# ScalarE's order of two instructions in the expert layers: the copy of the fifth product and the cast of the first activation block

## Chip, cores and metric

One core of a Trainium2 chip runs the whole program. The metric is the device time of one execution in microseconds (us), lower is better.

## The reference

Attention over 4 batches, 8 heads, 768 positions and head size 64, with 4 sink positions and a window of 128, gives 3072 rows `x` of 512 columns. A soft assignment of rows to 8 experts (`P`, eight rounds of row and column scaling) weighs what the experts make of every row:

```python
for e in range(E):                 # 8 experts
    h = np.maximum(x @ w1[e], 0.0) # 512 -> 1024
    ye = h @ w2[e]                 # 1024 -> 512
    out += P[:, e:e + 1] * ye
```

## The kernel before, in words

Every matrix product is made in pieces: an operand is split into a rounded part and the rest, and three of the four partial products are summed in PSUM. The expert layers run over the 3072 rows in three parts of 1024. The first part is interleaved with other work; the second and third part, from 938 us on, are the loop that the change touches. There the work is cut into 32 units for each part (8 experts, 4 slices of 256 hidden columns), so 64 units in all, and both layers use a scheme with seven products of blocks (M1 to M7) in place of eight.

The order is written by hand. `unit` (L1339) goes through the list `STEPS2`, and `tick` runs one step at a time:

```python
STEPS2 = ["M2", "M1", "M5", S_, "M3", S_, "M6", S_, S_, "M7", S_, S_, "M4", S_]
```

Steps are counted from 0 below. A step with a product's name is six matmuls of the first layer (`product`, L721) into one of two PSUM tiles. M2, M5 and M3 go to the tile `c2`, and M3 adds to what M5 left there; M1, M6, M7 and M4 go to `c1`. A step `S_` is a step of the second layer (L1269) with products made of earlier units' activations: six matmuls, or three where a group of one unit is worked on (group [0] and [1] at the start of each part; unit 3 takes two such steps in each `S_`).

What follows a product is issued in `after`. After M2, M5 and M3, ScalarE copies `c2` to SBUF (`copied`, L1215, tiles M). After M1, M6 and M7, VectorE adds that copy to `c1` (L1219, `summed`), applies relu and the expert's weight (L1220) and so makes the activation blocks A11, A21 and A22 in tiles `w`; after M4 it makes A12 (L1249). GpSimd makes three more blocks S3, S1, S2, S4 out of these by sums and differences (L1238, L1242, L1243, L1251; the last makes S4 in the place of A11, one step into the next unit).

Each of the seven blocks is then split into `hf` tiles for the second layer by `form` and `piece`: ScalarE casts the block (L746), and one step later VectorE subtracts the cast from the block (L747). `form(steps, ...)` sets by `at` how many steps after the current one the cast is issued; what is due at a step is issued ahead of the step's own work, in the order in which it was put on the list. S4's cast, put on the list in step 12 of a unit with 5 steps, comes due in step 3 of the next one.

Engines work through their own instructions in the order in which they are issued. M3's first matmul writes `c2` and so waits until ScalarE has copied M5 out of it.

Of the kernel before, what the change touches and what calls it, by code (L numbers as in the profile page):

```python
# [220 lines left out]
def tile_sink_attention_moe(ctx: ExitStack, tc: tile.TileContext, q, k, v, wg, w1, w2, out):  # L221
# [496 lines left out]
    def product(ps, w1, x, start, stop):  # L718

        for j, (a, k, b) in enumerate(TERMS):  # L720
            nc.tensor.matmul(ps, lhsT=w1(a, k), rhs=x[:, b, k, :], start=(start and j == 0),  # L721
                             stop=(stop and j == len(TERMS) - 1), skip_group_check=not start)
# [9 lines left out]
    def at(steps, f):  # L732
        due.setdefault(clock[0] + steps, []).append(f)
# [10 lines left out]
    def piece(dst, src, then=None):  # L744

        nc.scalar.copy(dst[:, 0], src)  # L746
        at(1, lambda: nc.vector.tensor_sub(dst[:, 1], src, f32(dst[:, 0])))  # L747
        if then:
            at(3, then)
# [392 lines left out]
    with ExitStack() as p1:  # L1142
# [12 lines left out]
        def load_w1(k):  # L1155
            for _ in range(k):
                key = next(coming1, None)
                if key:
                    part, n, m = key
                    t = W1Q[key] = w1p.tile([P, 2, KH, P], F32R, name="W1q")  # L1160
                    nc.sync.dma_start(f32(t).rearrange("p w k f -> p w (k f)"), w1s[units1[n]][:, FA[W1_OF[m]]])
# [28 lines left out]
        def load_form(m):  # L1190
            fm = READS[m]
            XF[fm] = (xpool if fm[0] == "B" else xtp).tile([P, 2, KH, HT], F32R, name=fm)
            nc.sync.dma_start(f32(XF[fm]), xfs[FORMS.index(fm)])
# [3 lines left out]
        def first2(part, n):  # L1197

            PB = PBS[part, units1[n][0]]
            T = {}  # L1200

            def run(m):
                c = "c2" if m in ("M2", "M5", "M3") else "c1"
                start = m in ("M2", "M1", "M5")
                if start:
                    T[c] = ps0.tile([P, HT], F32, name=c)
                W = W1Q.pop((part, n, m))
                product(T[c], lambda a, k: W[:, a, k, :], XF[READS[m]], start, True)
                at(1, lambda: load_w1(1))
                if (part, n) == (1, NJ - 1):  # L1210
                    at(1, lambda: load_form(m))

            def copied(m):
                t = T[m] = cp.tile([P, HT], F32, name=m)
                nc.scalar.copy(t, T["c2"])  # L1215

            def summed(key, m, th):
                w = T[key] = wp.tile([P, HT], F32, name="w")
                nc.vector.tensor_add(w, T["c1"], T[m])  # L1219
                nc.vector.scalar_tensor_tensor(w, w, 0.0, PB[:, th], op0=ALU.max, op1=ALU.mult)  # L1220

            def form(steps, fm, src):
                def f():
                    t = F[part, n, fm] = hp.tile([P, 2, HT], F32R, name="hf")
                    piece(t, src)

                at(steps, f)

            def after(m):
                if m in ("M2", "M5", "M3"):  # L1230
                    copied(m)
                elif m == "M1":
                    summed("A11", "M2", 0)
                    form(1, "A11", T["A11"])
                elif m == "M6":
                    summed("A21", "M3", 1)
                    S3 = wp.tile([P, HT], F32, name="w")
                    nc.gpsimd.tensor_sub(S3, T["A11"], T["A21"])  # L1238
                    form(2, "S3", S3)
                elif m == "M7":  # L1240
                    summed("A22", "M5", 1)
                    nc.gpsimd.tensor_add(T["A21"], T["A21"], T["A22"])  # L1242
                    nc.gpsimd.tensor_sub(T["A11"], T["A21"], T["A11"])  # L1243
                    form(2, "S1", T["A21"])
                    form(3, "A22", T["A22"])
                    form(4, "S2", T["A11"])
                else:
                    w = wp.tile([P, HT], F32, name="w")
                    nc.vector.scalar_tensor_tensor(w, T["c1"], 0.0, PB[:, 0], op0=ALU.max, op1=ALU.mult)  # L1249
                    form(1, "A12", w)  # L1250
                    at(3, lambda: nc.gpsimd.tensor_sub(T["A11"], w, T["A11"]))  # L1251
                    form(5, "S4", T["A11"])

            return run, after
# [156 lines left out]
```

## Time and profile before

| what | value |
|---|---|
| time, median of 3 runs (lowest to highest) | 2230.27 us (2229.29 to 2231.7) |
| the profiled execution's own time | 2228.16 us |
| its span in the trace | 2226.4 us |
| TensorE's mean granted clock, share of 2.4 GHz | 0.996 |
| busy share of the span: TensorE matmul, weight load, VectorE, ScalarE, GpSimd | 98%, 80%, 71%, 40%, 33% |
| mean HBM traffic | 204 GB/s |

The profiled execution is one run; 1.8 us of its time lie outside the span. Busy shares are means over stages that differ; a matmul's end is modelled, so how long a step takes is read from the starts of the steps that follow each other.

### The profile page before, as it was taken

How to read it: one execution, taken by the hardware profiler on the slowest of the kernel's cores; microseconds unless marked ns; L12 is line 12 of the kernel's file. 1: busy time of each engine (PE TensorE's matmuls, PEld its weight loads, DVE VectorE, ACT ScalarE, POOL GpSimd, SP SyncE). 2: the span in 40 equal slices, each digit the busy share in tenths (PEclk: the TensorE clock that was granted, in tenths of full speed). 3: DMA queues.
4: the chain of work that ended last, by engine and by line, in shares of the span. 5: the costliest groups of instructions: out<-in, count | busy, mean ns of one | idle time of the engine just before them, and what ended most of it. 6: DMA issues, size and time to landing. Idle time of an engine off the chain costs nothing. (4 is left out here: it accounts for less than half of the span.)

```text
span 2226.4 us, 31975 instructions
## 1 busy us (share of the span) xinstructions
PE 2176.1 (98%) x10525; PEld 1770.8 (80%) x10525; DVE 1580.4 (71%) x2941; ACT 889.9 (40%) x1908; POOL 727.0 (33%) x947
## 2 busy tenths in 40 slices
PE   7999998999999999999999999999999999999998
PEld 5888886788888888767888888888778888888886
DVE  8878868687777777767666666666766666666666
ACT  7777753344444444432223333232332333322232
POOL 7655632233233233022222223322222223232221
PEclk9999998999999999999999999999999999999999
DMA  6333325599989989876666666667856666666662
GB/s 173 85 83 82 89 64 175 186 311 298 295 292 305 297 290 304 272 250 194 190 198 200 195 190 200 203 189 253 290 171 197 200 195 190 200 204 190 199 190 82
DMA packets 396635, 454.88 MB, mean 204 GB/s; under 512 B 99696, under 2 KB 263728, under 8 KB 395568
## 3 DMA queue, kind: packets, MB, share of 16 engines
q1 hardware_dynamic: 396464, 452.77, 65.5%
q8 instruction: 86, 1.41, 0.3%
q14 instruction: 85, 0.70, 0.1%
HBM read 315.21 MB, written 137.46 MB: 203 GB/s over the span
## 5 line engine op out<-in xcount | busy, mean ns | idle before, releaser
L746 ACT CAST hf<-w 128x512 fp32r<-128x512 f32 x448 | 271.9, 621 | 722.2 <-POOL w L1238 307.4
L1269 PE MATMUL o<-hf,W2q 128*128 128x512 f32 x1920 | 479.5, 392 | 3.5 <-ACT w L1327 1.7
L1269 PEld LDWEIGHTS o<-hf,W2q 128*128 128x128 f32 x1920 | 359.9, 188 | 84.5 <-DVE acc L1280 2.7
L747 DVE TENSOR_TENSOR hf<-w,hf 128x512 fp32r<-128x512 f32 x448 | 334.0, 762 | 84.6 <-ACT hf L746 71.5
L721 PE MATMUL c<-T,W1q 128*128 128x512 f32 x1536 | 391.7, 390 | 1.7 <-DVE w L1219 1.7
L721 PEld LDWEIGHTS c<-T,W1q 128*128 128x128 f32 x1536 | 287.7, 188 | 65.8 <-DVE w L1219 3.4
L1280 DVE TENSOR_TENSOR acc<-o,acc 128x512 f32<-128x512 f32 x320 | 219.7, 687 | 152.7 <-PE o L1269 152.6
L721 PE MATMUL c<-B,W1q 128*128 128x512 f32 x1152 | 292.3, 397 | 8.5 <-DVE w L1249 3.9
L721 PEld LDWEIGHTS c<-B,W1q 128*128 128x128 f32 x1152 | 210.8, 188 | 78.0 <-ACT M L1215 27.4
L1238 POOL TENSOR_TENSOR w<-w 128x512 f32<-128x512 f32 x64 | 83.0, 1297 | 552.8 <-DVE w L1220 552.8
L1219 DVE TENSOR_TENSOR w<-c,M 128x512 f32<-128x512 f32 x192 | 132.1, 688 | 169.9 <-PE c L721 168.1
L1269 PE MATMUL held<-hf,W2q 128*128 128x512 f32 x768 | 197.8, 392 | 1.2 <-DMA W2q<-w2s 1.2
L721 PE MATMUL c<-T,W1f 128*128 128x512 f32 x672 | 173.3, 394 | 0.0
L992 PE MATMUL o<-W2f,h 128*128 128x512 f32 x672 | 171.4, 391 | 0.8 <-DVE acc L999 0.8
L992 PE MATMUL held<-W2f,h 128*128 128x512 f32 x672 | 171.9, 390 | 0.0
L1269 PEld LDWEIGHTS held<-hf,W2q 128*128 128x128 f32 x768 | 144.1, 188 | 32.5 <-DMA W2q<-w2s 1.6
L1215 ACT COPY M<-c 128x512 f32<-128x512 f32 x192 | 112.2, 585 | 137.9 <-PE c L721 137.9
L1251 POOL TENSOR_TENSOR w<-w 128x512 f32<-128x512 f32 x64 | 107.2, 1675 | 175.4 <-DVE hf L747 175.4
L721 PEld LDWEIGHTS c<-T,W1f 128*128 128x128 f32 x672 | 127.1, 190 | 28.7 <-DVE C L964 0.7
L992 PEld LDWEIGHTS o<-W2f,h 128*128 128x128 f32 x672 | 126.0, 188 | 28.7 <-DVE acc L999 1.2
L992 PEld LDWEIGHTS held<-W2f,h 128*128 128x128 f32 x672 | 126.1, 188 | 26.6
L1242 POOL TENSOR_TENSOR w<-w 128x512 f32<-128x512 f32 x64 | 82.9, 1295 | 184.9 <-DVE w L1220 182.1
(187 smaller groups left out, 3059.8 us busy)
## 6 DMA issues: line engine op xcount, KB each, us to landing
W1q<-w1s SPq DMA_DIRECT2D x448, 256.0 KB
W2q<-w2s SPq DMA_DIRECT2D x448, 256.0 KB
w1s<-W1f SPq DMA_DIRECT2D x56, 896.0 KB
w2s<-WT SPq DMA_DIRECT2D x136, 256.0 KB
r<-in_moe_w_dram SPq DMA_DIRECT2D x64, 512.0 KB
w2s<-W2f SPq DMA_DIRECT2D x56, 256.0 KB
PB<-psd SPq DMA_DIRECT2D x16, 512.0 KB
w2s<-W2f SPq DMA_DIRECT2D x56, 128.0 KB
```

The lines of the kernel that those rows point to most:

```text
L721: nc.tensor.matmul(ps, lhsT=w1(a, k), rhs=x[:, b, k, :], start=(start and j == 0), stop=(stop and j == len(TERMS) - 1), skip_group_check=n ...
L746: nc.scalar.copy(dst[:, 0], src)
L747: at(1, lambda: nc.vector.tensor_sub(dst[:, 1], src, f32(dst[:, 0])))
L992: nc.tensor.matmul(o, lhsT=h[c, th][:, a, off:off + P], rhs=W2F[n][:, w, c, :], start=(begin and c == 0 and j == 0), stop=(end and c == 1 ...
L1215: nc.scalar.copy(t, T["c2"])
L1219: nc.vector.tensor_add(w, T["c1"], T[m])
L1238: nc.gpsimd.tensor_sub(S3, T["A11"], T["A21"])
L1242: nc.gpsimd.tensor_add(T["A21"], T["A21"], T["A22"])
L1251: at(3, lambda: nc.gpsimd.tensor_sub(T["A11"], w, T["A11"]))
L1269: nc.tensor.matmul(o, lhsT=W2Q[part, n, m][:, a, k * P:(k + 1) * P], rhs=F[part, n, H_OF[m]][:, w, :], start=(j == 0 and (begin or not hol ...
L1280: nc.vector.tensor_add(sums[m, k], o, sums[m, k])
```

## The change

```diff
@@ def after(m): @@
                 elif m == "M1":
                     summed("A11", "M2", 0)
-                    form(1, "A11", T["A11"])
+                    form(2, "A11", T["A11"])
```

A11 is made after M1 (step 1). Its cast on ScalarE comes due in step 3 instead of step 2, and VectorE's subtraction in step 4 instead of step 3. The change holds for all 64 units; nothing is added or taken out.

On ScalarE, unit 16 of the second part, from the copy of M2 to the copy of M3. `w_13625` is A11 of this unit, `w_13455` is S4 of the unit before, `c2` is the PSUM tile. Before:

```order
L746 CAST hf_13592<-w_13585 128x512
L1215 COPY M2_13613<-c2_13606 128x512
L746 CAST hf_13630<-w_13625 128x512
L1215 COPY M5_13639<-c2_13632 128x512
L746 CAST hf_13641<-w_13455 128x512
L1215 COPY M3_13659<-c2_13632 128x512
```

With the change:

```order
L746 CAST hf_13592<-w_13585 128x512
L1215 COPY M2_13613<-c2_13606 128x512
L1215 COPY M5_13637<-c2_13630 128x512
L746 CAST hf_13639<-w_13455 128x512
L746 CAST hf_13641<-w_13625 128x512
L1215 COPY M3_13659<-c2_13630 128x512
```

The cast of A11 moved past the copy of M5 and past the cast of S4, and now stands just ahead of the copy of M3.

On VectorE, the same unit, from A11's sum (L1219, L1220) to A21's. Before:

```order
L1219 TENSOR_TENSOR w_13625<-c1_13618,M2_13613 128x512
L1220 SCALAR_TENSOR_TENSOR w_13625<-w_13625,PB_13120 128x512
L747 TENSOR_TENSOR hf_13630<-w_13625,hf_13630 128x512
L747 TENSOR_TENSOR hf_13641<-w_13455,hf_13641 128x512
L1280 TENSOR_TENSOR acc_11171<-o_13663,acc_11171 128x512
L1219 TENSOR_TENSOR w_13681<-c1_13618,M3_13659 128x512
```

With the change:

```order
L1219 TENSOR_TENSOR w_13625<-c1_13618,M2_13613 128x512
L1220 SCALAR_TENSOR_TENSOR w_13625<-w_13625,PB_13120 128x512
L747 TENSOR_TENSOR hf_13639<-w_13455,hf_13639 128x512
L747 TENSOR_TENSOR hf_13641<-w_13625,hf_13641 128x512
L1280 TENSOR_TENSOR acc_11171<-o_13663,acc_11171 128x512
L1219 TENSOR_TENSOR w_13681<-c1_13618,M3_13659 128x512
```

The subtraction for A11 moved behind that for S4; both now stand in step 4, ahead of the second layer's addition of step 5 (L1280).

## Rows read from the trace of the kernel before

**Rows 1.** The page: busy time of each engine, share of the span, instructions.
```profile
PE 2176.1 (98%) x10525; PEld 1770.8 (80%) x10525; DVE 1580.4 (71%) x2941; ACT 889.9 (40%) x1908; POOL 727.0 (33%) x947
```
**Rows 2.** Busy time by stretch, 28 units of the second part: us, busy (instructions), granted clock.
```profile
core 0: us, PE busy (x) PEld busy (x) DVE busy (x) ACT busy (x) POOL busy (x), PEclk, DMA share, GB/s
1015.90:1560.00 544.10, 544.10 (x2354) 439.48 (x2353) 363.09 (x533) 162.27 (x280) 155.94 (x112) 1.00 0.66 203
```
**Rows 3.** Who waited for whom, weight loads, whole span: us, times, longest us.
```profile
PEld c L721 <- ACT M L1215: 28.2, 64, 1.1
```
**Rows 4.** Who waited for whom, matmuls, 760 to 2200 us.
```profile
PE c L721 <- ACT M L1215: 1.8, 4, 0.7
```
**Rows 5.** Timeline, unit 16: start us, duration us, engine, line [idle before <-releaser].
```profile
1249.08 2.88 PE L721 MATMUL c<-B,W1q 128*128 128x512 f32 x12
...
1250.50 1.67 POOL L1251 TENSOR_TENSOR w<-w 128x512 f32<-128x512 f32 x1 [2.43 <-DVE hf L747]
1250.69 0.59 ACT L1215 COPY M<-c 128x512 f32<-128x512 f32 x1 [0.81 <-PE c L721]
1251.57 1.32 PEld L721 LDWEIGHTS c<-T,W1q 128*128 128x128 f32 x6
1251.80 1.52 PE L721 MATMUL c<-T,W1q 128*128 128x512 f32 x6
...
1253.15 1.53 PE L1269 MATMUL held<-hf,W2q 128*128 128x512 f32 x6
1253.52 0.62 ACT L746 CAST hf<-w 128x512 fp32r<-128x512 f32 x1 [2.24 <-DVE w L1220]
1254.04 0.58 ACT L1215 COPY M<-c 128x512 f32<-128x512 f32 x1
1254.17 0.69 DVE L747 TENSOR_TENSOR hf<-w,hf 128x512 fp32r<-128x512 f32 x1 [0.69 <-ACT hf L746]
1254.52 0.62 ACT L746 CAST hf<-w 128x512 fp32r<-128x512 f32 x1
1254.67 1.23 PEld L721 LDWEIGHTS c<-B,W1q 128*128 128x128 f32 x6 [0.41 <-ACT M L1215]
1254.67 1.66 PE L721 MATMUL c<-B,W1q 128*128 128x512 f32 x6
...
1256.17 1.53 PE L1269 MATMUL o<-hf,W2q 128*128 128x512 f32 x6
1256.42 0.59 ACT L1215 COPY M<-c 128x512 f32<-128x512 f32 x1 [1.28 <-PE c L721]
...
1257.74 0.69 DVE L1280 TENSOR_TENSOR acc<-o,acc 128x512 f32<-128x512 f32 x1 [1.88 <-PE o L1269]
...
1258.92 2.91 PE L1269 MATMUL o<-hf,W2q 128*128 128x512 f32 x12
1259.19 0.69 DVE L1219 TENSOR_TENSOR w<-c,M 128x512 f32<-128x512 f32 x1 [0.76 <-PE c L721]
...
1261.67 0.62 PE L721 MATMUL c<-T,W1q 128*128 128x512 f32 x2
```
**Rows 6.** Timeline, last unit of the third part.
```profile
2179.15 1.54 PE L1269 MATMUL o<-hf,W2q 128*128 128x512 f32 x6
...
2180.67 1.23 PEld L721 LDWEIGHTS c<-B,W1q 128*128 128x128 f32 x6 [0.41 <-ACT M L1215]
```
**Rows 7.** Timeline of PE, units 1 and 2 of the second part.
```profile
965.35 1.56 PE L721 MATMUL c<-B,W1q 128*128 128x512 f32 x6
966.74 0.86 PE L1269 MATMUL o<-hf,W2q 128*128 128x512 f32 x3
...
981.72 0.86 PE L1269 MATMUL o<-hf,W2q 128*128 128x512 f32 x3
983.24 1.65 PE L721 MATMUL c<-B,W1q 128*128 128x512 f32 x6 [0.66 <-ACT M L1215]
```
**Rows 8.** Timeline of PE, unit 3 of the second part.
```profile
999.43 0.85 PE L1269 MATMUL held<-hf,W2q 128*128 128x512 f32 x3
...
1001.20 1.66 PE L721 MATMUL c<-B,W1q 128*128 128x512 f32 x6 [0.24 <-ACT M L1215]
1002.70 0.63 PE L1269 MATMUL o<-hf,W2q 128*128 128x512 f32 x2
```

## Prediction

> **What bounds the kernel now.** The page's engine line comes first: TensorE has matmuls in flight for 98% of the span and no other engine is busy for more than 80% [rows 1]. In 28 units of the second part the matmul time fills the stretch to the last hundredth, at a granted clock of 1.00, which is the 2.4 GHz level [rows 2]; by that view nothing is left to win. But a matmul's end is modelled, so I go to the starts. The 28 units take 544.10 us, 19.43 us each.
>
> The list of waits names a cause. TensorE's weight loads waited 64 times, 28.2 us together, for ScalarE's copy of a product (L1215) [rows 3], while the matmul row of the same pair shows 1.8 us in 4 waits [rows 4]. Which of the two is the loss has to come from the timeline of one unit [rows 5]. The reader should follow four step starts there. M2 and M1 are two product steps, 1249.08 to 1251.80: 1.36 us each. Two second-layer steps, 1258.92 to 1261.67, are 1.38 us each. So a second-layer step and a product step should be 2.74 us together. The pair that contains M3 goes from 1253.15 to 1256.17: 3.02 us. **0.28 us are lost there in each unit**: M3 starts 1.52 us after the step ahead instead of 1.38 (0.14), and its own step takes 1.50 instead of 1.36 (0.14).
>
> Why it starts late stands beside it. M3's first weight load starts at 1254.67 and waited for the copy of M5. That copy ran from 1254.04 for 0.58 us. It was ready sooner, but ScalarE was at the cast of A11, which waited for VectorE's L1220 and started at 1253.52. An instruction that nobody needs soon stands ahead of one that TensorE waits for.
>
> **The change, part by part.** The diff adds and removes no instruction and no transfer. It moves 64 casts (ScalarE) and the 64 subtractions behind them (VectorE) by one step; the queue of the DMAs (SyncE) keeps its order.
>
> *The copy of M5.* Without the cast ahead of it, it waits for M5's last matmul alone. Two rows price that wait: M3's copy starts at 1256.42, when M3's step has given way to the next at 1256.17, so 0.25 us later; M2's copy starts at 1250.69, and M2's step ended at 1249.08 + 1.36 = 1250.44, again 0.25. For M5 that is 1253.15 + 0.25 = 1253.40, 0.64 earlier than now. The copy takes 0.59, to 1253.99; from a copy's end to the weight load that waits for it are 0.05 us (1254.62 to 1254.67), so the load may start from 1254.04. In undisturbed steps it starts 0.23 ahead of its matmul (1251.57 for 1251.80). M3 should start at 1253.15 + 1.38 = 1254.53, its load at 1254.30. **The copy is 0.26 us early, so all 0.28 us come back.** The kernel has a twin of this place already: M2, one step between, then M5, which also waits for a copy out of `c2`; M5's first load at 1251.57 shows no wait [rows 5].
>
> *How many units.* The last unit of the third part shows the same 0.41 us of idle ahead of the load, and M3 again 1.52 us behind the step ahead [rows 6]. Each part has three units that differ, 1 to 3; the other 29 of each part show 0.14 us of late start within 0.01. So 58 x 0.28 = 16.2 us.
>
> *Unit 2* has a short second-layer step of three matmuls between M5 and M3, from 981.72; M3 starts at 983.24 [rows 7]. The new copy runs from 981.97 to 982.56, the load and M3 go at 982.61: 0.63 us won, and a part of the wait stays. The third part repeats it: 2 x 0.63 = 1.3 us. *Unit 3*: step from 999.43, M3 at 1001.20, end 1002.70 [rows 8], so 3.27 us for 2.74: 0.53 lost. The copy would end at 1000.27, with 0.05 to the load 1000.32; the load's place is 1000.58, so all comes back: 2 x 0.53 = 1.1 us. *Unit 1* shows no such loss (M3 at 965.35, next step 1.39 later [rows 7]): nothing.
>
> *The cast of A11, one step later.* It costs ScalarE nothing new. After the copy of M5 come the cast of S4 and that of A11. S4's sum on GpSimd is done at 1250.50 + 1.67 = 1252.17, so both casts run at once, 0.6 us each, from 1253.99 to 1255.2; M3's copy has its product at 1256.1 and finds ScalarE idle (it sat idle 1.28 us before that copy [rows 5]). The second layer first reads a unit's A11 in the next unit or later, so nobody waits for the cast.
>
> *The subtraction on VectorE.* 0.69 us move into step 4, where the next work is the addition L1280 at 1257.74, ahead of which VectorE sat idle for 1.88 us for want of TensorE's result [rows 5]. That idle time covers it and 1.2 us remain. If the cover were gone, L1280 would be late; its tile `o` has a second buffer, so it is next written in the second of the two steps from 1258.92, at 1260.3, and the addition now ends at 1258.43: 1.9 us more.
>
> *The sum.* 16.2 + 1.3 + 1.1 = 18.6 us, taken as 18.5. Unknown is how much another wait gives back. Ends for it: nothing, as for M5 after M2's copy, and 2 us, if the few waits in units 1 to 3, where ScalarE also copies second-layer sums, shift by as much as the two kinds of unit above lose (1.3 + 1.1, rounded). I take nothing, since 58 of 64 units are of the first kind. The starts are read to 0.01 us, so 0.28 may be 0.26 to 0.30, or 1.2 us either way in all. The profiled execution took 2228.16 us, and would take 2209.7. The median of the runs stands 2.1 us above it: **2211.8 us.**
>
> **A rule weighed against a row.** M3's first weight load starts with its matmul at 1254.67, not 0.23 ahead of it as elsewhere [rows 5], so the wait holds the load too, and the step behind it is 0.14 us long. The Trainium skill, "TensorE: Matmul & The Clock Gate", section "Step-by-step: what each phase is for", says that TensorE pulls weight loads ahead of matmuls in flight when they go to the background buffer. By that rule the weights would lie ready during the wait, and the 0.14 us in M3's own step would have another cause that the change does not touch. The row speaks against it here.
>
> **Rivals.**
> *Only the late start comes back.* If M3's 1.50 us were a property of its operands, 58 x 0.14 = 8.1, with 1.3 and 2 x 0.39 = 0.8 from units 2 and 3, would be won: 10.2 us, 2220.1. For it: the long steps are all M3's. Against: M2 and M1 read B blocks too at 1.36, and M3 of unit 1, which did not wait, took 1.39 [rows 7]. The rule of the Trainium skill just named belongs here. Chance 0.06.
> *TensorE is full already.* If matmul busy time were the truth, only its 1.8 us of waits could be won [rows 4]: 2228.5. Against: equal steps at equal clock that differ by 0.14. A chance of 0.04, with the case that some new wait eats the gain.
> *Slower: M3's copy becomes the late one.* The cast of A11 and that of S4 now both stand ahead of M3's copy, whose result VectorE adds at 1259.19 for A21 [rows 5]. If GpSimd's S4 came late, both casts and the copy would queue behind it, A21 would be late, and M7, which needs `c1`, with it. S4 would have to end after 1256.1 - 1.2 = 1254.9 instead of 1252.17 for the copy to be late at all, 2 us beyond that for A21's sum to feel it, and 1.5 beyond that for M7, due at 1261.67, when A21's sum has read `c1` by 1259.9. That makes 2.7 + 2 + 1.5 = 6.2 us; at 7.2, 1 us in each unit, less the 0.28: 64 x 0.7 = 45 us, 2275. Against: S4 stood ahead of M3's copy before too, and 2.7 us are a wide margin. Chance 0.02.
> *The change does nothing.* ScalarE's order as built shows the copy ahead of both casts; I give this none of its own.
>
> **How the numbers follow.** The forecast has a chance of 0.88. Its range: 18.6 and 1.2 more, or 1.2 + 2 less, and about 1 us for where the median of three runs falls, so 2209.0 to 2216.0; this alone holds eight in ten, the rivals lie outside. A measurement of this kernel tells 0.2%, 4.5 us, from no change. Faster by more: 0.88 + 0.06 = 0.94; within: 0.04; slower: 0.02.
>
> **What would show it.** In the profile after, the wait of weight loads for L1215 falls from 28.2 us in 64 waits to under 3 us in a few, those of unit 2. Twenty-eight units take 28 x 19.15 = 536 us. In one unit M5's copy starts 0.25 us after the next step begins, two casts follow it back to back, and M3's load starts 0.23 us ahead of its matmul. I would be wrong if the load waited for something else at the same place, if M3's step stayed at 1.50, or if the units stayed at 19.43 with the wait gone.

## The result, and the profile after

| | before | with the change |
|---|---|---|
| median of the runs (lowest to highest) | 2229.78 us of 4 (2226.2 to 2231.7) | 2208.2 us of 4 (2207.69 to 2211.3) |
| profiled execution, its span | 2228.16 us, 2226.4 us | 2211.3 us, 2209.6 us |

The ratio is 0.9912, with a 95% interval of 0.9900 to 0.9924: the change makes the kernel faster by 17 to 22 us. The forecast was 2211.8 us, the range 2209.0 to 2216.0. The direction and the place were right; the median lies 0.8 us under the range's lower end.

The time came back where M3 waited. This is the changed kernel's timeline of the unit shown in [rows 5] (start us, duration us, engine, line, idle before):

```profile
1246.66 2.88 PE L721 MATMUL c<-B,W1q 128*128 128x512 f32 x12
...
1249.38 1.52 PE L721 MATMUL c<-T,W1q 128*128 128x512 f32 x6
...
1250.74 1.54 PE L1269 MATMUL held<-hf,W2q 128*128 128x512 f32 x6
1250.99 0.59 ACT L1215 COPY M<-c 128x512 f32<-128x512 f32 x1 [2.13 <-PE c L721]
1251.48 1.14 ACT L746 CAST hf<-w 128x512 fp32r<-128x512 f32 x2
1251.89 1.32 PEld L721 LDWEIGHTS c<-B,W1q 128*128 128x128 f32 x6
1252.11 1.52 PE L721 MATMUL c<-B,W1q 128*128 128x512 f32 x6
1252.13 1.29 DVE L747 TENSOR_TENSOR hf<-w,hf 128x512 fp32r<-128x512 f32 x2 [1.06 <-ACT hf L746]
...
1253.47 1.54 PE L1269 MATMUL o<-hf,W2q 128*128 128x512 f32 x6
1253.73 0.59 ACT L1215 COPY M<-c 128x512 f32<-128x512 f32 x1 [1.11 <-PE c L721]
...
1255.05 0.69 DVE L1280 TENSOR_TENSOR acc<-o,acc 128x512 f32<-128x512 f32 x1 [1.62 <-PE o L1269]
```

The copy of M5 starts 0.25 us after the step behind M5 begins (1250.74, 1250.99) and ends at 1251.58. M3's first load starts at 1251.89, 0.22 ahead of its matmul and without a wait. From 1250.74 to 1253.47 the pair with M3 takes 2.73 us, where it took 3.02. Both casts follow the copy as one row, both subtractions as another, ahead of the addition L1280, for which VectorE still sits idle for 1.62 us.

The same over 28 units, unit 4 to 31 of the second part, answers to [rows 2]:

```profile
core 0: us, PE busy (x) PEld busy (x) DVE busy (x) ACT busy (x) POOL busy (x), PEclk, DMA share, GB/s
1017.06:1552.80 535.74, 535.74 (x2354) 441.57 (x2353) 361.85 (x533) 162.52 (x280) 155.99 (x112) 1.00 0.67 205
```

That is 19.13 us a unit instead of 19.43, at the same granted clock of 1.00. Matmul busy time fills both stretches to the last hundredth, 544.10 of 544.10 us and 535.74 of 535.74, while 1.5% of the time vanished. The Trainium skill says in "Perfetto Trace Analysis", section "Identifying the Most-Contended Engine", that matmul busy time is a bad measure of how close a kernel is to its limit, and names the share of the peak arithmetic rate and the busy share of weight loads to use instead. The trace agrees: matmul busy time shows nothing of the gain, while the busy share of weight loads rose from 80.8% (439.48 of 544.10) to 82.4% (441.57 of 535.74).

The waits of weight loads for L1215, 28.2 us in 64 before [rows 3], are all but gone. Of the 64, 62 were M3's first load and two were M5's in unit 2; the four that are left are M5 and M3 in unit 2 of each part. The largest waits of first-layer loads in the loop now belong to other lines, with 5.6 and 3.4 us already there before (us, times, longest):

```profile
PEld c L721 <- DVE w L1249: 5.6, 4, 1.4
...
PEld c L721 <- DVE w L1219: 3.5, 5, 1.3
...
PEld c L721 <- ACT M L1215: 1.7, 4, 0.5
```

One part of the profile after is chance. This execution took 3 us more than the other three, and its timeline shows where: the first twelve matmuls of the second part took 5.46 us, not about 3, while the first weights of that part were landing.

```profile
937.78 5.46 PE L721 MATMUL c<-B,W1q 128*128 128x512 f32 x12 [2.81 <-DMA W1q<-w1s]
```

The next profile of the same kernel did not repeat it (unit 0 took 20.7 us there, 21.0 before the change, 23.5 here). Nor does it go with ScalarE's order: unit 0 lies between 20.7 and 23.5 us in the twelve profiles below, and took 22.5 in E2, whose order on ScalarE is that of before. To keep such things out, the profiles are compared below from the first matmul of M2 in unit 1 of the second part to the end of the span, a stretch that holds 63 of the 64 units.

| kernel | span | M2 of unit 1 | from there to the end |
|---|---|---|---|
| before | 2226.4 | 959.0 | 1267.4 |
| changed | 2209.6 | 961.3 | 1248.3 |
| changed, second profile | 2206.7 | 958.9 | 1247.8 |
| changed, third profile | 2208.0 | 959.9 | 1248.1 |
| E1 copy first only | 2206.3 | 958.3 | 1248.0 |
| E2 subtraction late only | 2226.0 | 958.5 | 1267.5 |
| E3 cast twice | 2266.6 | 959.3 | 1307.3 |
| E4 half a cast first | 2212.6 | 958.9 | 1253.7 |
| E5 S1 later | 2205.6 | 960.5 | 1245.1 |
| E6 A11 after M3's copy | 2206.4 | 957.9 | 1248.5 |
| E7 S3 later | 2206.1 | 961.2 | 1244.9 |
| E8 S1, S3, A12 later | 2198.5 | 959.4 | 1239.1 |

The changed kernel repeats within 0.5 us in the last column ("the column" from here on), so differences of 1 us can be read in it.

### The profile page after: what moved, and what is told of

The parts are those of the page before. It is cut to its first block, busy times and chain, and to the rows that moved or that the text cites. A ratio compares the mean times of both kernels' runs of the same rounds, so it can differ in the third digit from the quotient of the medians.

```text
span 2209.6 us, 31976 instructions
## 1 busy us (share of the span) xinstructions
PE 2161.0 (98%) x10525; PEld 1777.6 (80%) x10525; DVE 1578.6 (71%) x2941; ACT 890.4 (40%) x1908; POOL 726.5 (33%) x947
## 5 line engine op out<-in xcount | busy, mean ns | idle before, releaser
L746 ACT CAST hf<-w 128x512 fp32r<-128x512 f32 x448 | 266.3, 622 | 580.1 <-POOL w L1238 306.6
L747 DVE TENSOR_TENSOR hf<-w,hf 128x512 fp32r<-128x512 f32 x448 | 328.7, 761 | 66.2 <-ACT hf L746 57.6
L1280 DVE TENSOR_TENSOR acc<-o,acc 128x512 f32<-128x512 f32 x320 | 220.0, 688 | 180.5 <-PE o L1269 180.3
L721 PE MATMUL c<-B,W1q 128*128 128x512 f32 x1152 | 286.5, 393 | 6.7 <-DVE w L1249 3.9
L721 PEld LDWEIGHTS c<-B,W1q 128*128 128x128 f32 x1152 | 217.1, 189 | 55.3 <-DVE w L1249 5.6
L1219 DVE TENSOR_TENSOR w<-c,M 128x512 f32<-128x512 f32 x192 | 132.3, 689 | 145.1 <-PE c L721 141.3
L1215 ACT COPY M<-c 128x512 f32<-128x512 f32 x192 | 112.9, 588 | 262.7 <-PE c L721 262.7
```

Of the source, the lines that this page charges most:

```text
L1280: nc.vector.tensor_add(sums[m, k], o, sums[m, k])
```

## Experiments

The theory: the cast of A11 ahead of the copy of M5 on ScalarE is the whole cause. The rivals: the move of the subtraction on VectorE did it, or M3's long step belongs to its operands. The two halves of the change were made alone first.

**E1: the copy first, nothing else.** The cast follows the copy in the same step, ahead of S4's cast; VectorE's order is that of before.

```diff
                 if m in ("M2", "M5", "M3"):
                     copied(m)
+                    if m == "M5":
+                        form(0, "A11", T["A11"])
                 elif m == "M1":
                     summed("A11", "M2", 0)
-                    form(1, "A11", T["A11"])
...
-                at(steps, f)
+                at(steps, f) if steps else f()
```

> Only ScalarE's order of the copy of M5 and the cast of A11 is exchanged; the cast follows the copy at once, ahead of S4's cast, and VectorE's subtraction stays in step 3 as before the change. Theory (the cast ahead of the copy is the whole cause): the same gain as the changed kernel, 18 to 21 us, so 2209 to 2212 us, M3's pair of steps 2.74 us. Rival (the move of the subtraction on VectorE, or A11 going behind S4, gives a part): less than 14 us of gain, above 2216 us.

2209.54 us, ratio 0.9911 (0.9894 to 0.9928), 1248.0 us in the column: all of the gain. The copy of M5 again ran without the cast ahead of it:

```profile
1247.94 0.59 ACT L1215 COPY M<-c 128x512 f32<-128x512 f32 x1 [2.13 <-PE c L721]
1248.42 1.14 ACT L746 CAST hf<-w 128x512 fp32r<-128x512 f32 x2
1248.84 1.32 PEld L721 LDWEIGHTS c<-B,W1q 128*128 128x128 f32 x6
```

**E2: the subtraction late, nothing else.**

```diff
-    def piece(dst, src, then=None):
+    def piece(dst, src, then=None, wait=1):
...
-        at(1, lambda: nc.vector.tensor_sub(dst[:, 1], src, f32(dst[:, 0])))
+        at(wait, lambda: nc.vector.tensor_sub(dst[:, 1], src, f32(dst[:, 0])))
...
-                    piece(t, src)
+                    piece(t, src, wait=2 if fm == "A11" else 1)
```

> Only VectorE's subtraction for A11 is moved one step later; ScalarE's order is that of before the change. Theory: no gain, 2230 us within 3 us, 64 waits of weight loads for the copy of M5 as before. Rival (the move on VectorE helps by itself): 5 us or more faster.

2227.77 us, ratio 0.9993 (0.9984 to 1.0003), and the same row of waits for L1215 as before the change:

```profile
PEld c L721 <- ACT M L1215: 28.2, 64, 1.1
```

The step is later in all 64 units, but VectorE's order differs only in the 32 whose step 3 has an addition for VectorE: there the subtraction now stands behind it. In the others, unit 16 among them, nothing lies between steps 3 and 4 on VectorE, and the order is that of before. E2 also leaves A11's subtraction ahead of S4's, which the change does not. What closes this is E1: its order on VectorE is that of before in every unit, and it has the whole gain. So no part of the gain needs the move on VectorE.

**E3: the cast twice.** If the copy's place is the cause, more work ahead of it must cost more.

```diff
                     t = F[part, n, fm] = hp.tile([P, 2, HT], F32R, name="hf")
+                    if fm == "A11":
+                        nc.scalar.copy(t[:, 0], src)
                     piece(t, src)
```

> The cast of A11 stands ahead of the copy of M5 as before the change, and is made twice (the second writes the same values). Theory: a second cast pushes the copy back by the 0.52 us that lie between the starts of a cast and of the copy behind it (1253.52, 1254.04), and as the load of M3 is late already, TensorE loses all of it: 0.80 us a unit instead of 0.28, 62 x 0.52 = 32 us more, 2262 us (2255 to 2268). Rival (M3's long pair of steps is a property of its operands, not of the copy): 2230 us within 3 us.

2268.54 us, ratio 1.0175 (1.0158 to 1.0192). The sign and the place are those of the theory; the size is 0.5 us over the end of what I expected, and the rows say why:

```profile
1262.50 1.54 PE L1271 MATMUL held<-hf,W2q 128*128 128x512 f32 x6
1262.86 0.62 ACT L1226 CAST hf<-w 128x512 fp32r<-128x512 f32 x1 [2.29 <-DVE w L1220]
1263.52 0.62 ACT L746 CAST hf<-w 128x512 fp32r<-128x512 f32 x1
1264.04 0.58 ACT L1215 COPY M<-c 128x512 f32<-128x512 f32 x1
...
1264.67 1.23 PEld L721 LDWEIGHTS c<-B,W1q 128*128 128x128 f32 x6 [1.07 <-ACT M L1215]
```

The second cast starts 0.66 us behind the first, not 0.52. It writes the same tile, and it starts only after the first has ended (1262.86 + 0.62 = 1263.48), where two casts into different tiles overlap by 0.10 us (1.14 us for two of 0.62 in E1). The load of M3 is that much later, and a unit takes 20.07 us (28 units in 561.90) instead of 19.43, 0.64 more.

**E4: half a cast ahead.** A dose between nothing and the whole.

```diff
                     t = F[part, n, fm] = hp.tile([P, 2, HT], F32R, name="hf")
-                    piece(t, src)
+                    if fm == "A11":
+                        nc.scalar.copy(t[:, 0, 0:HT // 2], src[:, 0:HT // 2])
+                        at(1, lambda: nc.vector.tensor_sub(t[:, 1], src, f32(t[:, 0])))
+                    else:
+                        piece(t, src)
...
                     copied(m)
+                    if m == "M5":
+                        t = F[part, n, "A11"]
+                        nc.scalar.copy(t[:, 0, HT // 2:], T["A11"][:, HT // 2:])
```

> The cast of A11 is cut in two: 256 of 512 columns ahead of the copy of M5, the rest behind it; the subtraction is where it was before the change. Theory: a half cast takes some 0.3 us of ScalarE ahead of the copy, so M3's load is about 0.17 us late instead of 0.37; the loss falls to between 0.05 and 0.15 us a unit: 8 to 15 us of gain, 2215 to 2222 us. A rival in which any cast ahead of the copy costs the whole wait gives 2230; one in which the 0.26 us of lead that I worked out are too small a figure gives 2210.

2214.46 us, ratio 0.9935 (0.9918 to 0.9951): 15.5 us of gain by the medians, half a microsecond past what I expected, 13.7 by the column, within it. The half cast takes 0.41 us and the copy starts 0.31 us behind its start:

```profile
1250.00 1.54 PE L1276 MATMUL held<-hf,W2q 128*128 128x512 f32 x6
1250.36 0.41 ACT L1226 CAST hf<-w 128x256 fp32r<-128x256 f32 x1 [2.24 <-DVE w L1220]
1250.67 0.58 ACT L1215 COPY M<-c 128x512 f32<-128x512 f32 x1
1251.15 0.41 ACT L1238 CAST hf<-w 128x256 fp32r<-128x256 f32 x1
1251.31 1.23 PEld L721 LDWEIGHTS c<-B,W1q 128*128 128x128 f32 x6 [0.20 <-ACT M L1215]
1251.37 1.59 PE L721 MATMUL c<-B,W1q 128*128 128x512 f32 x6
```

The four kernels make one scale. M3's first load is due 1.15 us behind the start of the step ahead of it (1250.74 to 1251.89 in the changed kernel). What it is late by, and what a unit takes over the changed kernel's 19.13 us:

| kernel | load late by | a unit, us | lost |
|---|---|---|---|
| changed | 0 | 19.13 | 0 |
| half a cast ahead | 1251.31 - 1251.15 = 0.16 | 537.69 / 28 = 19.20 | 0.07 |
| before | 1254.67 - 1254.30 = 0.37 | 19.43 | 0.30 |
| cast twice | 1264.67 - 1263.65 = 1.02 | 20.07 | 0.94 |

TensorE loses what the load is late by, less 0.07 to 0.09 us. The copy of M5 sets M3's start, and what stands ahead of that copy on ScalarE is paid for on TensorE.

**E6: the cast still later**, behind the copy of M3.

```diff
-                    form(2, "A11", T["A11"])
+                    form(4, "A11", T["A11"])
```

(The line with minus is the changed kernel's.)

> The cast of A11 two steps later still than in the changed kernel, behind the copy of M3, its subtraction in step 6. Theory (nobody waits for this cast, and M3's copy is early enough with or without it): the time of the changed kernel within 2 us. Rival (the cast ahead of M3's copy holds something up, or a later cast is late for GpSimd's work in the place of A11): 3 us or more off.

2207.84 us, 0.9909 (0.9892 to 0.9925), 1248.5 us in the column: the same as the changed kernel. Nobody waits for the cast of A11, in step 3 or in step 5, and it holds nothing up ahead of M3's copy. The changed kernel itself, beside it:

> The changed kernel again, beside the two that follow. Theory: 19 to 22 us faster than the kernel before, 2208 to 2211 us; 28 units of the second part in 535.7 us as in its first profile. In the first profile unit 0 took 2.6 us longer than before because the first weights' transfers landed later; if that is chance, this profile does not repeat it, if the change makes it, it does.

2207.99 us, 0.9909 (0.9892 to 0.9925).

**E5: the same idea at the next wait.** In the changed kernel the largest wait of matmuls inside the loop was for A12's L1249, in units 2 and 3 of each part. VectorE does L1249 behind the subtraction for S1, which waits for S1's cast and so for GpSimd.

```diff
-                    form(2, "S1", T["A21"])
+                    form(3, "S1", T["A21"])
```

> The changed kernel, with the cast of S1 one step later too (form 3 instead of 2), so that VectorE's subtraction for S1, which waits for that cast and so for GpSimd, no longer stands ahead of A12's L1249. In units 2 and 3 of each part the first load of M1 waited for L1249, 5.6 us in 4 waits. Theory: those four waits go, some 4.5 us, about 2204 us. Rival (the weights' product M4 or GpSimd sets the pace there, and another wait takes the place): 2208 us within 1.5 us.

2208.06 us, 0.9911 (0.9895 to 0.9928): by the medians nothing, and the 4.5 us that I expected did not come. In the column, 1245.1 us, 2.7 to 3.2 us are won. The four waits for L1249 are gone, but a second queue of the same kind lay behind them, here in unit 2:

```profile
977.79 1.30 POOL L1243 TENSOR_TENSOR w<-w 128x512 f32<-128x512 f32 x1
977.81 2.92 PE L721 MATMUL c<-B,W1q 128*128 128x512 f32 x12
...
979.12 1.14 ACT L746 CAST hf<-w 128x512 fp32r<-128x512 f32 x2 [0.23 <-POOL w L1243]
980.16 0.58 ACT L1278 COPY acc<-o 128x512 f32<-128x512 f32 x1
980.64 0.59 ACT L1215 COPY M<-c 128x512 f32<-128x512 f32 x1
...
981.28 1.23 PEld L721 LDWEIGHTS c<-T,W1q 128*128 128x128 f32 x6 [0.97 <-ACT M L1215]
981.28 1.66 PE L721 MATMUL c<-T,W1q 128*128 128x512 f32 x6 [0.55 <-ACT M L1215]
```

The copy of M2 stands behind the casts of S2 and A12 and a second-layer copy, and M5 waits for it. Over both parts the weight loads' waits for L1215 rose from 1.7 us in 4 to 4.0 us in 6, the new ones at M5 in units 2 and 3. So the theory and its rival were each right in part: the waits went, and about a third of the 4.5 us (1.3 to 1.8) came back at the next product. This span also began its second part 1.6 us later than that of the changed kernel run beside it (M2 of unit 0 at 939.8 and 938.2), which hides a part of the gain in the total.

**E7 and E8: the queues taken one by one.** E7 is the changed kernel with S3's cast one step later; E8 has S1's too, and A12's two steps later, behind the next unit's copy of M2. The first pair of lines is E7, all three are E8; the lines with minus are the changed kernel's.

```diff
-                    form(2, "S3", S3)
+                    form(3, "S3", S3)
...
-                    form(2, "S1", T["A21"])
+                    form(3, "S1", T["A21"])
...
-                    form(1, "A12", w)
+                    form(3, "A12", w)
```

> The changed kernel once more, beside the two that follow: 2206 to 2211 us; from M2 of unit 1 of the second part to the end of the span 1247.8 to 1248.3 us, as in its two profiles so far (1267.4 before).

> The changed kernel with the cast of S3 one step later (form 3 instead of 2). In units 1 to 3 that cast waits for GpSimd and stands ahead of ScalarE's copies of second-layer sums (matmul waits of 0.6 us each on L1278, two) and, through its subtraction, ahead of VectorE's L1219 for A22 (two waits of 0.8 to 0.9 us). Theory, the same as for the copy of M5: these four waits go and TensorE gains 3 to 4 us from M2 of unit 1 to the end: about 1244.5. Rival (GpSimd sets the pace and the wait comes back at another product, as it did in part when S1 was cast later): under 1 us of gain.

> The changed kernel with S3's and S1's casts one step later and A12's two steps later, so behind the next unit's copy of M2. When S1 alone was later, M1's waits for L1249 went and M5 waited for M2's copy instead, which stood behind the casts of S2 and A12; 2.7 us were won from M2 of unit 1 to the end. Theory: with A12 behind that copy most of that second wait goes too, about 1 us, and with S3's 3 to 4 us it comes to 6 to 8 us under the changed kernel: 1240 to 1242 us from M2 of unit 1 to the end, some 2201 us in all. Rival (the gains overlap, or a wait returns): 1244 or more.

The changed kernel: 2209.82 us, 0.9911 (0.9898 to 0.9925). E7: 2207.12 us, 0.9898 (0.9883 to 0.9913), in the column 3.2 us under the changed kernel, as expected in size. The four waits went, but a part of the rival came too: S3's subtraction now stands ahead of an addition L1280 behind M7 in unit 3, and second-layer matmuls wait for that addition, 1.2 us in 2 waits that the changed kernel does not have. E8: **2201.47 us, 0.9878 (0.9863 to 0.9893)**, the fastest kernel of the study; its interval lies wholly under the changed kernel's. By the medians it is 8.4 us under the changed kernel, in the column 9.0, 1 us more than I had worked out; 0.9 of the 9.0 lie behind the start of the last unit (50.6 us against 51.5), a stretch in which the changed kernel's own profiles differ by 0.7 us. What is left of matmul waits from 760 to 2200 us in E8 has no wait for L1249, L1219 or L1278 in it, of which the changed kernel had 3.9, 1.7 and 1.3 us:

```profile
PE c L721 <- DMA W1q<-w1s: 3.4, 3, 2.9
PE o L1269 <- ACT w L1327: 1.5, 1, 1.5
PE o L1269 <- DVE acc L1280: 1.3, 2, 0.7
PE held L1269 <- DMA W2q<-w2s: 0.5, 1, 0.5
```

Two short waits for transfers of first-layer weights are new (0.5 us; 1 wait before, 3 here), and so are the two for L1280, which E7 has too.

## Why the prediction was right, and where it was off

*The cause.* The step that the forecast rests on held: the cast stood ahead of the copy of M5, and taking it away returned the whole loss. E1 shows the order of the two on ScalarE to be enough, with VectorE's order untouched; E2, with the later subtraction alone, gains nothing; E3 and E4 show that the loss follows how late the copy is.

*The copy's new start.* Worked out: 0.25 us behind the next step's start, load free 0.26 us early. Measured: 0.25 (1250.74, 1250.99); the copy ends at 1251.58, and the load at 1251.89 shows no wait, so 0.31 us of lead, of which 0.05 went to the signal: 0.26.

*The size in a unit* was the term that was read too small. I took 0.28 us, from four starts in one unit, each read to 0.01. Measured is 0.30 (544.10 less 535.74, over 28): the pair with M3 fell from 3.02 to 2.73 us, 0.29, not to the 2.74 that I had put together from two other pairs. Over 58 units that is 1 us of the gain.

*Units 2 and 3.* Forecast 1.3 + 1.1 = 2.4 us for both parts. From M2 of unit 1 to M2 of unit 4 the second part went from 56.87 to 55.74 us, 1.1; the third part from unit 0 to unit 4 from 80.82 to 79.18, 1.6, of which 0.3 are unit 0's: 1.3. Together 2.4. The residue in unit 2 of the second part came out within a hundredth, M3 0.90 us behind the step's start (0.89 forecast); in the third part it is 0.84:

```profile
984.04 0.85 PE L1269 MATMUL o<-hf,W2q 128*128 128x512 f32 x3
984.94 1.66 PE L721 MATMUL c<-B,W1q 128*128 128x512 f32 x6
```

*The total.* From M2 of unit 1 on, 1267.4 to 1248.3 makes 19.1 us, and 0.3 for unit 0: 19.4 against 18.5. The medians are 21.6 us apart, 2 us more than the traces. That is within the spread: the runs of before lie 5.5 us apart and those of the change 3.6, and the two later pairs of medians, each with the kernel before run beside the changed one, are 20.1 us (2228.05, 2207.99) and 18.5 us (2228.28, 2209.82) apart. The forecast also went from a median of before, 2230.27, that a fourth run lowered to 2229.78. So the 3.6 us between forecast and result are 1 us of the size in a unit, 0.5 us of that median and some 2 us of spread. The range's lower end does not follow from its own working: 2230.3 less 18.6, 1.2 and 1 is 2209.5, not 2209.0.

*The rivals.* "Only the late start comes back" fell: M3's own step is 1.36 us now (1252.11 to 1253.47), so its length did belong to the wait, and the weight load was not pulled ahead of the matmul in the late cases: it started with it before the change (both at 1254.67) and in the kernel with two casts, 0.06 us ahead with half a cast, and 0.22 ahead where nothing was late. "TensorE is full already" fell with the 28 units. The slower case, M3's copy becoming late, did not come up: ScalarE sat idle for 1.11 us ahead of that copy, and E6, which takes the cast from there, has the same time. The new cover held as well: VectorE had 1.62 us of idle left ahead of L1280, where I had put 1.2; the two subtractions, now back to back, end 2.68 us behind the start of the step behind M5 (1250.74 to 1253.42), where they ended 2.71 behind it before (1253.15 to 1255.86), so they took nothing from that idle time.

## What to carry to other kernels

An engine works in order, so ask of each instruction who waits for it and how soon: one that nobody needs for many steps should not stand ahead of one that TensorE needs next, above all if the first has a wait of its own. Read the loss from the starts of steps, since matmul busy time can be full while 1.5% is lost, and look for a twin of the place elsewhere in the loop that shows what it costs undisturbed. Where one such wait is taken away, look for the next instruction in the same queue: one cast moved alone gave back part of its gain, three moved together won 8 to 9 us.

## What the runs showed of the hardware

A late weight load costs TensorE nearly all of its lateness: 0.16, 0.37 and 1.02 us late cost 0.07, 0.30 and 0.94 us. Some 0.08 us are free each time, and the list of weight loads shows more than either, 0.20, 0.41 and 1.07 us a wait, so a wait in that list is longer than the loss. I had also not expected that a cast that writes the same tile as the one before it starts 0.66 us behind it, just after its end, where a copy or a cast to another tile starts 0.52 behind, before its end.
